# q and k loaded in quadrants of two heads, and transposed with an output step of two words

## The chip, the cores and the metric

The kernel runs on one core of a Trainium2 chip. The core has five engines with instruction queues of their own: TensorE (PE, matmuls; its weight loads are listed apart as PEld), VectorE (DVE), ScalarE (ACT), GpSimd (POOL) and SyncE (SP, which here only issues stores). Sixteen DMA engines move data between the chip's memory and the core's SBUF. Each engine runs its queue in order and waits at an instruction until what it needs is there. The metric is the device time of one execution in microseconds.

## What is computed

The reference is an attention with a sliding window and a bias by distance, followed by a gated layer.

```python
# q, k, v: (8 batches, 8 heads, 576 tokens, 64), float32
scores = scale * q @ k.T                      # scale = 1/8
bias   = slopes[h] * -abs(i - j)              # slopes[h] = 2 ** -(h + 1)
mask   = (i - j >= 0) & (i - j < 128)
attn   = softmax(where(mask, scores + bias, -1e9))
x      = (attn @ v).transpose(0, 2, 1, 3).reshape(4608, 512)
H = maximum(x @ w_h, 0)
T = sigmoid(x @ w_t + b_t)
out = T * H + (1 - T) * x                     # (4608, 512), float32
```

## The kernel before

**Units and blocks.** The attention is done in 32 *units* (b, s, g): a batch b, a set s of four of the eight heads, and a half g of the token range. The gated layer is done in 36 *blocks* of 128 rows and 512 columns; a block (b, 4) collects the first 64 tokens of two neighbouring batches.

**The order** is written out: the string ORDER has one letter for each step, and every engine's queue is filled in the order of that string. The steps of attention are L (a load, POOL issues it), T (a transpose of a loaded q or k tile, DVE, L184), s (scores, PE, L227), e (exponential, ACT, L244), m (multiplication by the mask, DVE, L249), p (probabilities times v, PE, L260, L268, L281) and n (division by the row sum, DVE, L294 and L295). Those of a block are x (transpose of x on PE, L321), c (its copy to SBUF, ACT, L326), h (projection with w_h, PE, L331), z (projection with w_t and a matmul that adds the bias, PE, L355 and L357) or w and y (bias copied by ACT, L368, then the projection alone, L372), r and u (relu and subtraction of x: r on ACT, L338, and u on DVE, L344, or both in one DVE step, L347), a (tanh, ACT, L377), t or k (to a gate, on ACT, L381, or DVE, L385), g (multiplication by the gate, DVE, L390), o or q (addition of x, on POOL, L394, or DVE, L399) and d (store, SP). S and M are the setup. The tuples RELU_ACT, GATE_DVE, BIAS_ACT and ADD_DVE say which blocks take which form, and LOADS in which order the 60 loads are issued.

**Loads.** All loads are issued by POOL and turn float32 into bfloat16 on the way. A load of q or k (L130) brings one batch and four consecutive heads: each of the 128 partitions holds one head's 18 consecutive tokens, in one piece of 4,608 bytes read. The tile has its own buffer out of 20. A load of v (L136) brings 128 tokens of 8 or 16 heads, in pieces of 64 numbers.

**Transposes.** Scores need q and k with the head dimension on the partitions. DVE transposes each tile in 18 squares of 32x32 words of 4 bytes (two bfloat16 numbers each). Square t takes token t of every partition's 18, so that its 32 results belong at words t, t + 18, t + 36 and so on of the output:

```python
out=TR[i % NTR][:]....rearrange("p (s t) -> p t s", t=NT),   # NT = 18
in_=LD[i % NLD][:].bitcast(U32).rearrange("p (t i) -> p t i", i=32)
```

**Masks.** The bias and the mask are applied in one of two ways. Most units multiply the exponentials by a table MT (step m). The units listed in MASK_PE have the distances added to the scores on PE instead (function distances, L209): four matmuls, one per head, of a scaled identity SI with a table of distances RB, each 128x128 with 384 or 448 columns; then m falls away.

**x.** The result of n is kept as x, two head sets after one another, with 64 numbers per head.

Of the kernel before, what the change touches and what calls it, by code (L numbers as in the profile page):

```python
# [11 lines left out]
NLD, NTR, NPB = 20, 12, 8  # L12


RELU_ACT = (0, 3, 5, 8, 9, 11, 12, 13, 17, 19, 20, 21, 26, 28)
GATE_DVE = (6, 7, 9, 15, 19, 23, 25, 26, 29, 32, 34)

LOADS = (0, 1, 3, 4, 6, 5, 2, 12, 11, 9, 13, 17, 10, 16, 8, 18, 7, 14, 21, 19, 15, 20, 22, 27, 26, 23, 25, 24, 29, 30, 31, 32, 33, 28, 34, 37, 39, 35, 40, 47, 38, 36, 43, 44, 45, 46, 48, 42, 41, 52, 56, 57, 50, 53, 58, 59, 51, 49, 55, 54)

BIAS_ACT = (8, 9, 14, 17, 20, 24, 30, 31, 32, 33, 34, 35)  # L20
ADD_DVE = (33, 35)

MASK_PE = (11, 14, 19)
# [3 lines left out]
    "SLLSMSLLLTLLTLs0LTLeLLTLMSms0Lp4LeLTLmLs0LTp6enLs0nLmx4Lex5Tp6cmcs0Lnz4b5eLTp6mas0tfnz4e"  # L27
    "Lh5mx6rh7cux5az6ucgtTp4oap6nLds0nLh4Th5eLx6x7uLrs0Tcz4Leumh5cmx6as0cuz7egTp4oh6anLtds0Lm"
    "rp4tLuez6ngz7gaoTtx6p4aLmdcs0x7eh6noTp4Ltds0cLnmh7euz4kw6gux5aos0Tch7eLdTp4Lynrs0akmp4w7"
    "eyugnh6oaTx4rs0LdtgLcgLp6gmx4Lz5cnex4oTp6cLds0unLz4eoTp6aLds0anoh5tTeh4dmz6rux7ah4kmcx5t"  # L30
    "p6ucgs0rnox5ez4TLdh6gLcmax7s0roTz5cw4Lgp6deuTyLts0naLaLgz4ueLTop6Tas0otdh5enh4dgux6oth7u"
    "cgx4w5dh6mctoyurTx4ap6dcms0z4euknh5agp6Ttos0th4neLduz6rmLLx7ap4mcs0np6egx4kh5nocs0ruLdx4"
    "gw5p6LmcyeuLnh4Tox6az7rmtLdp4ags0cgz7otneTz6odTx4aLds0cx5mah4w7uh6cgkeuyoup4gtds0maz6eon"
    "x7Tp4dcs0nh7eTh4h5autmp6rgs0uz5oenx4mdp6cs0uakz4engx5p6macs0onx4z5cdmeh4ggp6aoux5nh4odct"
    "z5krmdw4h6gauox7tx5uycgdkh6gaocx4h7ucodw6p4utydnw7ygagow6p4aytnodh7agdtx6ox4uh5ckw7dh6gc"
    "uoyw5uygdaqh4akdgtuogdqd"
# [36 lines left out]
def kernel(  # L73
# [38 lines left out]
    LD = [cp.tile([P, NT * D], BF16, name=f"ld{i}") for i in range(NLD)]  # L112
# [11 lines left out]
    RB = cp.tile([P, 448], BF16, name="rb")  # L124
    PS = pp.tile([P, 8, 512], F32, name="ps")

    def load(kind, *at):
        if kind == "t":
            b, s, w = at
            nc.gpsimd.dma_start(  # L130
                out=LD[(4 * b + 2 * s + w) % NLD][:],
                in_=(q, k)[w][b, 4 * s : 4 * s + 4].rearrange("h (p t) d -> (h p) (t d)", t=NT))
        elif kind == "v":
            b, n, m = at
            rows, h = min(P, S - m * P), b % 2 * H
# [320 lines left out]
```

## Time and profile before

| | |
|---|---|
| time, median of 3 runs | 151.55 us (150.25 to 152.34) |
| the profiled execution: time, span of its instructions | 151.79 us, 150.1 us |
| granted TensorE clock, mean | 0.987 of full speed |
| loads by the software DMA queue | 42,960 packets, 15.21 MB written |
| read from memory, written to it | 30.41 MB, 9.44 MB |
| q and k: 32 loads, landing after issue | 4.1 to 12.1 us, median 7.4 |
| wait of transposes for loads | 4.7 us in 5 waits, all before 31 us |

The span runs from the first to the last instruction; the time is 1.69 us longer. A page of the profile gives busy times of engines, the span in 40 slices, the chain of work that ended last (followed back from the last instruction, at each step to what released it or to the instruction before it on its engine), and groups of instructions by line with the mean duration of one and the idle time of the engine ahead of them. Lines such as L184 are lines of the kernel's file.

### The profile page before, as it was taken

How to read it: one execution, taken by the hardware profiler on the slowest of the kernel's cores; microseconds unless marked ns; L12 is line 12 of the kernel's file. 1: busy time of each engine (PE TensorE's matmuls, PEld its weight loads, DVE VectorE, ACT ScalarE, POOL GpSimd, SP SyncE). 2: the span in 40 equal slices, each digit the busy share in tenths (PEclk: the TensorE clock that was granted, in tenths of full speed). 3: DMA queues.
4: the chain of work that ended last, by engine and by line, in shares of the span. 5: the costliest groups of instructions: out<-in, count | busy, mean ns of one | idle time of the engine just before them, and what ended most of it. 6: DMA issues, size and time to landing. Idle time of an engine off the chain costs nothing.

```text
span 150.1 us, 5788 instructions
## 1 busy us (share of the span) xinstructions
PE 130.9 (87%) x2525; PEld 80.3 (54%) x2525; DVE 132.2 (88%) x226; ACT 119.3 (80%) x167; POOL 87.9 (59%) x102
## 2 busy tenths in 40 slices
PE   0477589969999999979999899997999999999960
PEld 0136465444666665655755556674557566555520
DVE  4974998759899999999969999999999999977882
ACT  5298369913999899769999979979799898899860
POOL 6977662195075851994159870859655035685640
PEclk9999999995999999999999999999999999999999
DMA  2999999999999999899999998399999121253544
GB/s 47 186 165 199 182 208 198 179 217 167 131 135 167 198 208 220 156 150 204 256 226 185 130 211 279 51 195 214 185 215 144 65 74 63 51 173 140 195 142 155
DMA packets 48233, 25.01 MB, mean 167 GB/s; under 512 B 38480, under 2 KB 39504, under 8 KB 48208
## 3 DMA queue, kind: packets, MB, share of 16 engines
q0 software_dynamic: 42960, 15.21, 96.6%
q1 hardware_dynamic: 5248, 9.44, 18.3%
q8 instruction: 19, 0.31, 0.9%
q14 instruction: 6, 0.05, 0.1%
HBM read 30.41 MB, written 9.44 MB: 266 GB/s over the span
## 4 chain that ended last, share of the span: by engine, by line
PE 46%; DVE 27%; DMA 17%; issue 3%; POOL 2%; ACT 2%; DVEq 0%; POOLq 0%; ACTq 0%
PE ps L331 14%; PE ps L355 8%; DMA va<-in_v_dram 8%; DVE x L295 6%; DVE p L249 6%; PE ps L372 6%; DMA ld<-in_q_dram 5%; DVE tr L184 5%; PE ps L227 5%; DMA ld<-in_k_dram 4%; PE ps L281 4%; DVE uu L390 3%; PE ps L321 3%; PE ps L260 3%; DVE uu L347 3%
## 5 line engine op out<-in xcount | busy, mean ns | idle before, releaser
L394 POOL TENSOR_TENSOR ot<-uu,x 128x512 f32<-128x512 bf16 x34 | 42.8, 1265 | 49.0 <-DVE uu L390 30.6
L244 ACT ACTIVATE p<-ps 128x1792 bf16<-128x1792 f32 (+1 forms) x32 | 50.0, 1562 | 12.2 <-PE ps L227 12.2
L184 DVE STREAM_TRANSPOSE tr<-ld 128x576 uint32<-128x576 uint32 x32 | 39.4, 1249 | 4.7 <-DMA ld<-in_q_dram 3.9
L331 PE MATMUL ps<-wH,xt 128*128 128x512 bf16 x144 | 37.3, 391 | 0.0
L249 DVE TENSOR_TENSOR p<-p,mt 128x1792 bf16<-128x1792 bf16 (+1 forms) x29 | 29.5, 1021 | 1.4 <-ACT p L244 1.4
L136 POOL DMA_DIRECT2D va<-in_v_dram x25 | 25.2, 1014 | 1.4 <-DMA ld<-in_q_dram 0.9
L295 DVE TENSOR_TENSOR x<-ps,rd 128x512 bf16<-128x512 f32 (+1 forms) x32 | 24.3, 758 | 1.3
L355 PE MATMUL ps<-wT,xt 128*128 128x512 bf16 x96 | 25.2, 386 | 0.0
L326 ACT COPY xt<-ps 128x512 bf16<-128x512 bf16 x36 | 21.0, 586 | 3.5 <-PE ps L321 3.3
L377 ACT ACTIVATE tt<-ps 128x512 f16<-128x512 f32 x36 | 21.5, 604 | 2.9 <-PE ps L372 1.6
L227 PE MATMUL ps<-tr,tr 32*64 32x192 bf16 (+2 forms) x1280 | 20.2, 248 | 1.3 <-DVE tr L184 1.3
L331 PEld LDWEIGHTS <-xt 128*128 128x128 bf16 x144 | 13.3, 100 | 14.3 <-issue 1.7
L227 PEld LDWEIGHTS <-tr 32*64 32x64 bf16 x1280 | 16.6, 112 | 6.6 <-DVE tr L184 2.9
L260 PE MATMUL ps<-va,p 128*128 128x65 bf16 x256 | 13.9, 198 | 4.7 <-DMA va<-in_v_dram 2.1
L260 PEld LDWEIGHTS <-p 128*128 128x128 bf16 x256 | 11.7, 100 | 9.4 <-DVE p L249 2.7
L347 DVE SCALAR_TENSOR_TENSOR uu<-ps,x 128x512 bf16<-128x512 f32 x22 | 14.9, 685 | 2.0 <-PE ps L331 1.8
L390 DVE TENSOR_TENSOR uu<-uu,tt 128x512 bf16<-128x512 bf16 x36 | 15.9, 454 | 0.2
L381 ACT ACTIVATE tt<-tt 128x512 f16<-128x512 f16 x25 | 15.7, 634 | 0.1
L321 PE MATMUL ps<-ident,x 128*128 128x128 bf16 x144 | 13.9, 224 | 2.0 <-DVE x L295 1.8
L321 PEld LDWEIGHTS <-x 128*128 128x128 bf16 x144 | 10.2, 99 | 8.7 <-issue 2.7
L281 PE MATMUL ps<-va,p 64*64 64x65 bf16 x448 | 14.7, 200 | 0.0
L355 PEld LDWEIGHTS <-xt 128*128 128x128 bf16 x96 | 8.2, 99 | 8.1 <-issue 0.8
(46 smaller groups left out, 116.8 us busy)
## 6 DMA issues: line engine op xcount, KB each, us to landing
out_dram<-ot SPq DMA_DIRECT2D x32, 256.0 KB, 4.1
ld<-in_q_dram POOLq DMA_DIRECT2D x16, 288.0 KB, 7.9
ld<-in_k_dram POOLq DMA_DIRECT2D x16, 288.0 KB, 7.2
va<-in_v_dram POOLq DMA_DIRECT2D x12, 256.0 KB, 7.7
va<-in_v_dram POOLq DMA_DIRECT2D x11, 128.0 KB, 7.9
out_dram<-ot SPq DMA_DIRECT2D x8, 128.0 KB, 2.8
wT<-in_moe_w_t_dram POOLq DMA_DIRECT2D x1, 512.0 KB, 8.9
wH<-in_moe_w_h_dram POOLq DMA_DIRECT2D x1, 512.0 KB, 10.8
```

The lines of the kernel that those rows point to most:

```text
L136: nc.gpsimd.dma_start(out=VA[b // 2][0:rows, h : h + n * H, m, 0:D], in_=v[b : b + n, :, m * P : m * P + rows].rearrange("b h p d -> p (b ...
L184: nc.vector.transpose(out=TR[i % NTR][:].rearrange("p s e -> p (s e)").bitcast(U32).rearrange("p (s t) -> p t s", t=NT), in_=LD[i % NLD][: ...
L227: nc.tensor.matmul(out=PS[r * D : r * D + D, bank + a, c0:c1], lhsT=KT[row : row + 32, k0 : k0 + D, e], rhs=QT[row : row + 32, q0 : q0 + c ...
L244: nc.scalar.activation(out=PB[i][:, :, 0:w], in_=PS[:, bank : bank + 4, 0:w], func=ACTF.Exp, scale=scale)
L249: nc.vector.tensor_tensor(out=p[:, :, 0:w], in0=p[:, :, 0:w], in1=MT[s][:, :, 448 - w : 448] if g else MT[s][:], op=ALU.mult)
L260: nc.tensor.matmul(out=PS[:, bank + o, a * E : a * E + E], lhsT=p[:, a, col : col + P], rhs=VA[b // 2][:, b % 2 * H + 4 * s + a, i, :], st ...
L295: nc.vector.tensor_tensor(out=X[b, g][:, s, :, 0:n, :], in0=av[:, :, 0:n, 0:D], in1=rd[:, :, 0:n, :].to_broadcast([P, 2, n, D]), op=ALU.mult)
L321: nc.tensor.transpose(out=XP[b, i][:, c * P : (c + 1) * P], in_=xchunk(b, i, c), identity=ident[:])
L331: nc.tensor.matmul(out=pa, lhsT=XT[b, i][:, c, :], rhs=wH[:, c, :], start=c == 0, stop=c == NC - 1)
L355: nc.tensor.matmul(out=pz, lhsT=xt[:, c, :], rhs=wT[:, c, :], start=c == 0, stop=False)
L377: nc.scalar.activation(out=tt[:], in_=PZ.pop((b, i)), func=ACTF.Tanh, scale=0.5)
L394: nc.gpsimd.tensor_tensor(out=like(ot[:], i), in0=like(UU.pop((b, i))[:], i), in1=xview(b, i), op=ALU.add)
```

## The change

From batch 2 on (NBW = 2) a load of q or k is made of two DMAs. Each brings two heads into one quadrant of 32 partitions: partition p of the quadrant gets, of both heads, the token pairs 2p and 2p + 1 of each run of 64 tokens, nine pairs per head, each pair a piece of 512 bytes read and 256 written. The buffers now hold both halves of the heads of a batch (10 buffers twice as long); half s of a buffer holds heads 2a + s in quadrant a. A load fills two quadrants, both halves, so each of a batch's transposes reads what two loads brought. In a square, the 32 results of a transpose lie two words apart. For batches 0 and 1 the pieces and the squares stay as they were, with heads 2a + s instead of 4s + a.

With this a head set s has the heads 2a + s; the v tiles and SI are indexed so, and x is kept with both sets beside one another, so that a block's 512 columns are contiguous.

The distances are added by up to 20 matmuls of 64x64 instead of four of 128x128, over those columns of each 64-row part that the scores use, and RB has 256 columns. Seven units instead of three use them, two of them the first two units. The lists give 11 blocks instead of 14 to r on ACT, 10 instead of 12 to w and y, 3 instead of 2 to q, and 11 to k as before. ORDER and LOADS are new throughout.

```diff
-NLD, NTR, NPB = 20, 12, 8
+NLD, NTR, NPB, NBW = 20, 12, 8, 2
-RELU_ACT = (0, 3, 5, 8, 9, 11, 12, 13, 17, 19, 20, 21, 26, 28)
-GATE_DVE = (6, 7, 9, 15, 19, 23, 25, 26, 29, 32, 34)
+RELU_ACT = (4, 6, 7, 8, 9, 10, 16, 23, 24, 25, 30)
+GATE_DVE = (4, 8, 9, 13, 15, 16, 19, 24, 29, 32, 33)
...
-BIAS_ACT = (8, 9, 14, 17, 20, 24, 30, 31, 32, 33, 34, 35)
-ADD_DVE = (33, 35)
-MASK_PE = (11, 14, 19)
+BIAS_ACT = (9, 13, 14, 19, 26, 30, 32, 33, 34, 35)
+ADD_DVE = (32, 33, 35)
+MASK_PE = (0, 1, 9, 11, 15, 16, 23)
...
-    LD = [cp.tile([P, NT * D], BF16, name=f"ld{i}") for i in range(NLD)]
+    LD = [cp.tile([P, NS, NT * D], BF16, name=f"ld{i}") for i in range(NLD // 2)]
...
             b, s, w = at
-            nc.gpsimd.dma_start(
-                out=LD[(4 * b + 2 * s + w) % NLD][:],
-                in_=(q, k)[w][b, 4 * s : 4 * s + 4].rearrange("h (p t) d -> (h p) (t d)", t=NT))
+            ld, src = LD[(2 * b + w) % (NLD // 2)], (q, k)[w][b]
+            if b < NBW:
+                nc.gpsimd.dma_start(
+                    out=ld[:, s, :],
+                    in_=src.rearrange("(h s) (p t) d -> s h p (t d)", s=NS, t=NT)[s])
+                return
+            for a in (2 * s, 2 * s + 1):
+                nc.gpsimd.dma_start(
+                    out=ld[32 * a : 32 * a + 32, :, :].rearrange("p s (t x) -> p (s t) x", x=2 * D),
+                    in_=src[2 * a : 2 * a + 2].rearrange("h (t p j) d -> p (h t) (j d)", p=32, j=2))
...
     def tr(b, s, w):
         i = 4 * b + 2 * s + w
-        nc.vector.transpose(
-            out=TR[i % NTR][:].rearrange("p s e -> p (s e)").bitcast(U32).rearrange(
-                "p (s t) -> p t s", t=NT),
-            in_=LD[i % NLD][:].bitcast(U32).rearrange("p (t i) -> p t i", i=32))
+        to = TR[i % NTR][:].rearrange("p s e -> p (s e)").bitcast(U32)
+        ld = LD[(2 * b + w) % (NLD // 2)][:, s, :].bitcast(U32)
+        if b < NBW:
+            nc.vector.transpose(out=to.rearrange("p (s t) -> p t s", t=NT),
+                                in_=ld.rearrange("p (t i) -> p t i", i=32))
+        else:
+            nc.vector.transpose(out=to.rearrange("p (t s j) -> p t j s", s=32, j=2),
+                                in_=ld.rearrange("p (t j i) -> p t j i", j=2, i=32))
...
     def distances(s, g, bank):
-        w = width(g)
-        for a in range(4):
-            nc.tensor.matmul(out=PS[:, bank + a, 0:w], lhsT=SI[:, 4 * s + a, :],
-                             rhs=RB[:, 448 - w : 448], start=True, stop=False,
-                             skip_group_check=True)
+        steps, parts = tiles(g)
+        for n, step in enumerate(steps):
+            for a0 in (0, 2):
+                for i, r in step:
+                    c0, c1, k0, q0 = parts[i, r]
+                    at = D + q0 - k0
+                    if k0 == D:
+                        c0, at = 0, 0
+                    for a in (a0, a0 + 1):
+                        row = a % 2 * D
+                        nc.tensor.matmul(
+                            out=PS[r * D : r * D + D, bank + a, c0:c1],
+                            lhsT=SI[row : row + D, 2 * a + s, row : row + D],
+                            rhs=RB[row : row + D, at : at + c1 - c0], start=n == 0,
+                            stop=False, tile_position=(row, r * D), skip_group_check=True)
...
-            X[b, g] = xp.tile([P, NS, 2, 6, D], BF16, name="x")
+            X[b, g] = xp.tile([P, 2, 6, NS, D], BF16, name="x")
...
-            out=X[b, g][:, s, :, 0:n, :], in0=av[:, :, 0:n, 0:D],
+            out=X[b, g][:, :, 0:n, s, :], in0=av[:, :, 0:n, 0:D],
```

## The prediction

> **What bounds the kernel now.** I read the page's busy times and slices first, then the busy times in stretches of 10 us, then the chain, and last the POOL queue in order of time.
>
> The page, on busy time and in 40 slices of 3.75 us (tenths busy):
>
> ```profile
> PE 130.9 (87%) x2525; PEld 80.3 (54%) x2525; DVE 132.2 (88%) x226; ACT 119.3 (80%) x167; POOL 87.9 (59%) x102
> ...
> PE   0477589969999999979999899997999999999960
> ...
> DVE  4974998759899999999969999999999999977882
> ...
> DMA  2999999999999999899999998399999121253544
> ```
>
> Three things are full at once. PE and DVE are, from slice 10 to slice 34, and the DMA engines are until slice 30. Busy time on PE overstates its work, so I price PE by the chain, where matmuls run back to back:
>
> ```profile
> 19.75 11.87 DMA va<-in_v_dram
> 31.67 0.30 PE ps L260 x4
> ...
> 80.27 0.65 PE ps L209 x4
> ...
> 83.33 0.53 PE ps L227 x40
> ...
> 108.14 0.86 PE ps L355 x4
> 109.00 0.22 PE ps L357
> ...
> 112.87 0.24 PE ps L260 x8
> 113.12 0.37 PE ps L281 x12
> ...
> 131.01 0.86 PE ps L331 x4
> ...
> 144.09 0.88 PE ps L331 x4
> ```
>
> Columns are start, length, what. PE waits for a load of v until 31.67, ends its last projection at 144.97, and a DVE and store tail ends the span at 150.1. A projection costs 0.86 (with a bias matmul 1.08), a unit of scores 0.53 or 0.47, a unit of p times v 0.61 (0.86 with the shared block), the transposes of a block 0.25 (0.22 to 0.33), four distance matmuls 0.65. By the groups of PE in 0 to 31.6 us, what is left at 31.67 is 34 h (29.2), 21 z (22.7), 12 y (10.4), 32 x (8.0), 26 s (13.0), 28 p (19.1) and 3 distances (2.0): **104.4 us of work in 113.3 us**. So PE stalls for only 8.9 us. The chain runs on DVE from 38.5 to 65 and from 90.5 to 104.3; by the same prices these stretches hold 24.6 us of PE work in 26.5 and 12.2 in 13.8. Relieving DVE there can give 3.5 us.
>
> **The change, part by part.**
>
> *Transposes.* Groups by form:
>
> ```profile
> L184 DVE STREAM_TRANSPOSE tr<-ld 128x576 uint32<-128x576 uint32 x32 | 39.4, 1249 | 4.7 <-DMA ld<-in_q_dram 3.9 <-DMA ld<-in_k_dram 0.9
> L249 DVE TENSOR_TENSOR p<-p,mt 128x1792 bf16<-128x1792 bf16 x16 | 17.3, 1080 | 0.9 <-ACT p L244 0.9
> L295 DVE TENSOR_TENSOR x<-ps,rd 128x512 bf16<-128x512 f32 x24 | 16.6, 692 | 1.0
> L295 DVE TENSOR_TENSOR x<-ps,rd 128x768 bf16<-128x768 f32 x8 | 7.7, 958 | 0.3
> ```
>
> The two forms of L295 give 266 ns for 256 more elements, 1.04 ns each, and 160 ns fixed. A transpose at this slope would take 759 ns; it takes 1249. Either its output step of 18 words costs the other 490 ns, or the operation itself does. With a step of two words 24 of the 32 fall between 0.54 us (the slope of DVE's memsets, 165 ns for 128 elements and 272 for 256, plus its fixed 58 ns) and 1.25 us (nothing gained; the step shrinks, so I see no reason for more). I take 0.72, near the L295 slope: 24 x 0.53 = 12.7 us off DVE, bounds 0 and 17.
>
> Two rules of the Trainium skill oppose each other here. "SBUF — State Buffer" (Door 1, on cachelines) has lines of 16 bytes and wants two hits in each; a step of two words gives two, and 24 transposes at the full rate would save what I took. "Vector Engine (DVE) Microarchitecture Reference" (5.2) gives the full rate only to runs of two adjacent words; a two-word step has none, and by this rule of the Trainium skill the transposes stay at 1249 ns, the first rival below. The row of 1249 ns agrees with both.
>
> *Masks and small moves.* Seven units instead of three get their mask on PE: 4 x 1.02 (between the two forms of L249, 1.08 and 0.95) = 4.1 us off DVE. Three relus move from ACT plus L344 (483 ns) to L347 (685): +0.6; one add moves from POOL: +0.7. DVE in all: 132.2 - 12.7 - 4.1 + 1.3 = **116.7 us**. ACT loses three relus (603 each) and two bias copies (596): -3.0. The new layout of x keeps sizes and types; I take it as nothing.
>
> *Distances on PE.* Twenty 64x64 matmuls instead of four of 128x128. Ends: half a unit of scores (40 small matmuls in 0.5), 0.25, and the old 0.65. I take 0.5, nearest to a unit of scores because the tiles may run side by side. Two of the seven lie before 31 us, in the DMA's shadow. What is left for PE from the first p of batch 1 on, by the new order: 34 h 29.2, 24 z 25.9, 10 y 8.8, 32 x 8.0, 25 s 12.5, 28 p 19.1, 5 distances 2.5: **106.0 us**.
>
> *Start.* That p waited for the 21st load and now for the 20th, with one q/k load fewer ahead (1.4 us). But PE had caught up only 1.49 us before, and has some 0.6 us more to do, at the start's slower pace: resume at 31.0 instead of 31.67.
>
> *Loads.* This is the part that can hurt. In the queue on POOL:
>
> ```profile
> 10.55 0.54 POOL L130 DMA_DIRECT2D ld<-in_q_dram  x1 [0.92 <-DMA ld<-in_k_dram]
> ...
> 31.01 4.33 POOL L136 DMA_DIRECT2D va<-in_v_dram  x4
> ```
>
> 24 loads become 48, each of 576 pieces of 512 bytes read and 256 written, where a load had 128 pieces. An issue takes 0.56 us with 128 pieces, 1.17 with the 2048 of a v load: by the line between, 0.70 with 576. POOL gets 24 x (1.40 - 0.57) = +20 us, less one add (1.27): about 107 of 147. Its idle time (49 us ahead of L394, 31 of it waiting for DVE) hides that as long as adds and loads are not queued behind one another. At 10.55 and every later stall of the start, the issue waits for the landing of the eighth DMA before it; with two DMAs per load that is four loads in flight, not eight, and adds queue behind the wait.
>
> Time on the DMA engines: consecutive landings at the start lie 1.3 to 1.7 us apart for q/k (I use 1.4), 0.9 for a v load of 1024 pieces, 14 ns a piece and engine (1024/16 = 64), up to 18 ns with 2048 pieces in 2.3 us. By bytes alone 512-byte pieces change nothing: 1.4. If a piece costs per byte as two v pieces, 72 x 36 ns = 2.6. I take 1.65, nearer the bytes, since a v piece exceeds its bytes' time (9.8 ns at q/k's rate, 8 rows of 4,608 bytes per engine in 1.4 us) by 4 to 8 ns and so one of 512 bytes takes 24 to 28, at 72 per engine 1.7 to 2.0, or 1.4 if the two overlap. That is +6 us over the run (0 to 29). "SBUF — State Buffer" (Door 1) of the Trainium skill has 189 GB/s for a DMA on 32 partitions; as an estimate from it, 0.295 MB would take 1.56 us a load, and no row here shows such a DMA.
>
> What hides it: the landings of 45 to 116 us leave about 9 us in which nothing is in flight or only one load's latency runs (93.4 to 100.4 and around 46). What is late next if the cover goes: each transpose of a batch now waits for both loads of its tensor, behind it stand DVE's masks, norms and gates, and PE's scores wait for it.
>
> **Sum.** 31.0 + 106.0 + stalls + tail 5.1. Of the old 8.9 us of stalls I take away DVE's 3.5 and the 1.4 of the DVE pieces at 85.8 to 87.7, and keep 4.0. Span 146.1; the profiled run had 151.79 for a span of 150.1, so 147.8; it stands 0.24 over the median, so **147.6** against 151.55, 2.6% faster. Two per cent (148.5 to 154.6) is about what a measurement of this kernel can tell from no change.
>
> **The rivals.**
> 1. *Transposes stay long* (the step is not their cost). DVE keeps 129.4 and its two stretches; only 4.1 us of masks are lighter, half of that on the chain, less 1.6 us of PE work: 150 to 152. For it: nothing in the trace separates step from operation, and the memsets of va with a step of 130 bytes (80 elements in 125 ns) show no penalty. Against: the 490 ns over the slope of other rows have no other visible source.
> 2. *Freed DVE time turns into other stalls* (ACT 90% busy in mid-run, POOL's longer queue): stalls stay near 8.9, 31.0 + 106.0 + 8.9 + 5.1 + 1.7 = 152.7, or 149 with half of it.
> 3. *The loads become the bound: slower.* The place is the queue of loads from 32 us to the last v, behind which, in the new order, 28 us of PE work (from the p of batch 6 that needs it) and the tail follow. The 9 us of slack are used up from 9/24 = 0.4 us extra per load; at +0.6 it is 5 us late, against the 4 us gained elsewhere, so about 153; at +1.2 it is 20 us late, 168. POOL's limit of eight works in the same way. For it: DMA busy 9 to slice 30, and landings 6 to 12 us after issue. Against: until 116 us few transposes waited (4.7 us, all at the start), and the new order issues batch 3 earlier.
>
> **How the numbers follow.** Forecast (145 to 148.5): 0.42. Rivals 1 and 2, within 2%: 0.13 and 0.14. Rival 3: 0.31, mostly 154.6 to 162. The range 144.5 to 159 leaves out the best end (transposes at 0.54, no stalls) and the far end of rival 3.
>
> **What will show it.** L184 in two kinds, 1.25 us x8 and near 0.7 x24; L130 with 56 issues, the new near 0.7 us; distances at 0.5 a unit; the chain nearly all PE after 31 us. Waits of the transposes for ld beyond the start, POOL waiting for DMAs in mid-run, or v landing after PE wants it would make the prediction wrong on the slow side; L184 unchanged would make it wrong towards no change.

## The result, and the profile after

The changed kernel takes 172.09 us, median of 4 runs (170.89 to 177.39), against 151.30 us for the kernel before, measured beside it (150.25 to 152.34). Run against run the ratio is 1.135, with a 95% interval of 1.123 to 1.146: 13.5% slower, where 2.6% faster was forecast and the range ended at 159. The profiled execution has a span of 169.2 us (before 150.1), at a granted clock of 0.97. Medians below hold all runs of a kernel; the ratios leave out disturbed executions, so that the two can differ by a per cent.

Busy times, slices (now of 4.23 us) and the queue of loads, from the page of the changed kernel:

```profile
PE 132.1 (78%) x2656; PEld 85.1 (50%) x2687; DVE 127.4 (75%) x221; ACT 117.5 (69%) x162; POOL 106.0 (63%) x124
...
PE   0405660799939996689979999999799999999960
...
DVE  3337009577918799558959999999998998898892
...
DMA  1799999999999999999969999999999811233536
...
q0 software_dynamic: 70992, 15.22, 146.9%
```

PE was nearly full from slice 10 on. It now has holes until slice 21 (89 us) and a smaller one at slice 29, DVE has two empty slices at 17 to 25 us, and the DMA engines have next to no slack until slice 31. The same bytes come in 70,992 packets instead of 42,960.

The chain that ended last, in order of time (start, length, what):

```profile
3.96 10.93 DMA ld<-in_q_dram
15.18 11.71 DMA va<-in_v_dram
27.17 12.60 DMA va<-in_v_dram
40.05 9.65 DMA va<-in_v_dram
...
63.29 1.48 issue
...
70.41 2.02 issue
...
84.91 1.02 issue
```

Before, too, loads of v handed over to one another, the last ended at 31.67 us, and PE worked from there. Now a load of q and three of v do, and the last of these holds PE until 49.70 us. From there to the end of the span it is 119.5 us; from 31.67 us in the kernel before it was 118.4. **What was lost lies before 50 us**; the lighter DVE shows as no gain behind it. The three pieces called "issue" are new as well: PE idle with nothing that the profile shows to wait for.

Groups by form (busy us, mean ns of one, then the idle time ahead of it), of the changed kernel:

```profile
L192 DVE STREAM_TRANSPOSE tr<-ld 128x576 uint32<-128x576 uint32 x24 | 17.7, 758 | 4.5 <-DMA ld<-in_q_dram 4.3 <-DMA va<-in_v_dram 0.2
...
L137 POOL DMA_DIRECT2D ld<-in_q_dram x24 | 16.0, 669 | 5.2 <-DMA va<-in_v_dram 3.1 <-DMA wH<-in_moe_w_h_dram 1.2 <-DMA ld<-in_k_dram 0.8
...
L189 DVE STREAM_TRANSPOSE tr<-ld 128x576 uint32<-128x576 uint32 x8 | 9.7, 1253 | 16.9 <-DMA ld<-in_q_dram 16.4 <-DMA ld<-in_k_dram 0.5
...
L397 DVE TENSOR_SCALAR tt<-tt 128x512 f16<-128x512 f16 x11 | 7.3, 664 | 0.7 <-ACT tt L389 0.7
```

The 24 short transposes take 758 ns and a new issue 669 ns, both close to their forecast. The eight long transposes of batches 0 and 1, which the change hardly touches, wait 16.4 us for loads of q.

### The profile page after: what moved, and what is told of

Read it like the earlier page. It is cut to its first block, busy times and chain, and to the rows that moved or that the text cites. A ratio compares the mean times of both kernels' runs of the same rounds, so it can differ in the third digit from the quotient of the medians.

```text
span 169.2 us, 6109 instructions
## 1 busy us (share of the span) xinstructions
PE 132.1 (78%) x2656; PEld 85.1 (50%) x2687; DVE 127.4 (75%) x221; ACT 117.5 (69%) x162; POOL 106.0 (63%) x124
## 3 DMA queue, kind: packets, MB, share of 16 engines
q0 software_dynamic: 70992, 15.22, 146.9%
## 4 chain that ended last, share of the span: by engine, by line
PE 54%; DMA 27%; issue 8%; DVE 7%; POOL 1%; ACT 0%; DVEq 0%; POOLq 0%
DMA va<-in_v_dram 20%; PE ps L343 15%; PE ps L367 11%; PE ps L243 7%; DMA ld<-in_q_dram 6%; PE ps L297 6%; PE ps L333 5%; PE ps L276 4%; PE ps L369 3%; PE ps L384 2%; DVE tr L192 2%; DVE uu L359 2%; DVE uu L402 1%; PE ps L223 1%; DVE ot L411 1%
## 5 line engine op out<-in xcount | busy, mean ns | idle before, releaser
L406 POOL TENSOR_TENSOR ot<-uu,x 128x512 f32<-128x512 bf16 x33 | 41.0, 1246 | 32.3 <-DVE uu L402 20.0
L343 PE MATMUL ps<-wH,xt 128*128 128x512 bf16 x132 | 36.1, 387 | 0.7 <-issue 0.2
L265 DVE TENSOR_TENSOR p<-p,mt 128x1536 bf16<-128x1536 bf16 (+1 forms) x25 | 27.7, 1110 | 1.5 <-ACT p L260 1.5
L367 PE MATMUL ps<-wT,xt 128*128 128x512 bf16 x88 | 27.3, 403 | 1.2 <-issue 0.4
L189 DVE STREAM_TRANSPOSE tr<-ld 128x576 uint32<-128x576 uint32 x8 | 9.7, 1253 | 16.9 <-DMA ld<-in_q_dram 16.4
L192 DVE STREAM_TRANSPOSE tr<-ld 128x576 uint32<-128x576 uint32 x24 | 17.7, 758 | 4.5 <-DMA ld<-in_q_dram 4.3
L137 POOL DMA_DIRECT2D ld<-in_k_dram x24 | 15.8, 662 | 6.8 <-DMA ld<-in_q_dram 3.5
L343 PEld LDWEIGHTS <-xt 128*128 128x128 bf16 x144 | 13.0, 99 | 12.9 <-issue 0.8
L137 POOL DMA_DIRECT2D ld<-in_q_dram x24 | 16.0, 669 | 5.2 <-DMA va<-in_v_dram 3.1
L359 DVE SCALAR_TENSOR_TENSOR uu<-ps,x 128x512 bf16<-128x512 f32 x25 | 16.9, 677 | 1.4 <-PE ps L343 0.8
L402 DVE TENSOR_TENSOR uu<-uu,tt 128x512 bf16<-128x512 bf16 x36 | 17.2, 485 | 0.2
```

What stands on the lines that cost most here:

```text
L137: nc.gpsimd.dma_start(out=ld[32 * a : 32 * a + 32, :, :].rearrange("p s (t x) -> p (s t) x", x=2 * D), in_=src[2 * a : 2 * a + 2].rearrang ...
L265: nc.vector.tensor_tensor(out=p[:, :, 0:w], in0=p[:, :, 0:w], in1=MT[s][:, :, 448 - w : 448] if g else MT[s][:], op=ALU.mult)
L343: nc.tensor.matmul(out=pa, lhsT=XT[b, i][:, c, :], rhs=wH[:, c, :], start=c == 0, stop=c == NC - 1)
L367: nc.tensor.matmul(out=pz, lhsT=xt[:, c, :], rhs=wT[:, c, :], start=c == 0, stop=False)
L406: nc.gpsimd.tensor_tensor(out=like(ot[:], i), in0=like(UU.pop((b, i))[:], i), in1=xview(b, i), op=ALU.add)
```

## The experiments

Ratios are against the kernel before measured beside each, with their 95% intervals. The first question was the start.

**a_contig.** The changed kernel, batches 0 and 1 with four consecutive heads per load.

```diff
-                    in_=src.rearrange("(h s) (p t) d -> s h p (t d)", s=NS, t=NT)[s])
+                    in_=src[4 * s : 4 * s + 4].rearrange("h (p t) d -> (h p) (t d)", t=NT))
```

> The changed kernel, but loads of q and k of batches 0 and 1 take four consecutive heads again (the heads of these two batches end up in another order, so the result isn't the reference's; all sizes and counts stay). Theory A: the time went at the start, because a load of every second head is cut into four rows of heads that don't follow one another, and lands late (the first load 9.3 us after its issue, before 4.1; the first p of batch 1 at 41 us instead of 31.7). Then the first load lands after about 4.1 us, PE resumes at 31 to 36 us, and the time falls from 172 to 156 to 163. Theory B: the start is late because of the quadrant loads that stand ahead of the v loads of batch 1, eight DMAs in flight at a time. Then the first load may land early, but PE still waits near 47 to 50 us, and the time stays above 167.

161.89 us, ratio 1.068 (1.048 to 1.087): **10.2 us of the loss go with one line of the load.** The first transpose on DVE's timeline, of the changed kernel and then of this one (start, length):

```profile
10.69 1.26 DVE L189 STREAM_TRANSPOSE tr<-ld 128x576 uint32<-128x576 uint32 x1 [4.70 <-DMA ld<-in_q_dram]
```

```profile
5.65 2.65 DVE L189 STREAM_TRANSPOSE tr<-ld 128x576 uint32<-128x576 uint32 x2
```

Both loads were issued at 1.33 us. With strided heads the first lands 9.3 us later, with consecutive ones 4.3 (4.1 in the kernel before). The p of batch 1 on PE's timeline, in the changed kernel and in this one:

```profile
41.13 0.41 PE L276 MATMUL ps<-va,p 128*128 128x65 bf16 x8
...
49.74 0.35 PE L276 MATMUL ps<-va,p 128*128 128x65 bf16 x4 [2.79 <-DMA va<-in_v_dram]
```

```profile
31.83 0.42 PE L276 MATMUL ps<-va,p 128*128 128x65 bf16 x8
...
38.92 0.28 PE L276 MATMUL ps<-va,p 128*128 128x65 bf16 x4 [1.26 <-DMA va<-in_v_dram]
```

The first p comes 9.3 us earlier, the one that waits for v 10.8.

**b_strided.** The other way round: the kernel before, with every second head in batches 0 and 1.

```diff
-                in_=(q, k)[w][b, 4 * s : 4 * s + 4].rearrange("h (p t) d -> (h p) (t d)", t=NT))
+                in_=((q, k)[w][b].rearrange("(h s) (p t) d -> s h p (t d)", s=NS, t=NT)[s] if b < 2 else
+                     (q, k)[w][b, 4 * s : 4 * s + 4].rearrange("h (p t) d -> (h p) (t d)", t=NT)))
```

> The kernel before, with only the loads of q and k of batches 0 and 1 taking every second head (the heads of these batches are in another order, so the result isn't the reference's). Theory A: the first load lands after about 9 us instead of 4.1, PE resumes 8 to 12 us later than 31.7, time 159 to 164. Theory B: nothing of this, 150 to 154.

160.96 us, ratio 1.076 (1.061 to 1.092). The eight loads alone cost the kernel before about what they cost the changed one (7.6% here, 6.7% between a_contig and the changed kernel). The stretch of 0 to 10 us (from, length, busy times, then clock, DMA share, GB/s), of the kernel before and of this one:

```profile
0.00:10.00 10.00, 3.31 (x47) 1.70 (x48) 7.09 (x19) 5.41 (x11) 8.37 (x19) 1.00 0.87 130
```

```profile
0.00:10.00 10.00, 1.65 (x4) 0.51 (x4) 3.60 (x16) 4.65 (x10) 7.29 (x16) 1.00 0.51 69
```

The load does not keep the DMA engines busier: their share falls to 0.51, and what they move to 69 GB/s. The queue's packets in the stretch of 4 to 6 us (number, MB, the time that they took as a share of 16 engines), of the kernel before and of this one, where the first four loads have been issued by 4.5 us:

```profile
q0 software_dynamic: 195, 0.38, 109.0%
```

```profile
q0 software_dynamic: 191, 0.13, 49.6%
```

As many packets move a third of the bytes, for 133 of the 191 are under 512 bytes (28 of 195 before). The whole run has 3,072 packets more, 384 per strided load, all under 512 bytes. What these small packets add to the delay was not tried apart from the gap.

The row of 0.51 fits a rule of the Trainium skill, "DMA: Bandwidth & Descriptors" (Why a DMA increments its semaphore by 16 and not by 1, on the number of engines): a DMA is spread over the largest number of engines, 16 at most, that divides the slowest dimension of both its patterns. Four strided heads cannot be merged with the 32 partitions of each, so that this dimension is 4, where consecutive heads make one of 128. By this rule of the Trainium skill a load would have a quarter of the engines, and two loads at once half of them, which is the size of the 0.51 and the 49.6%. No run here names the engines or shows how many loads move at a time.

**a_quadbig.** The changed kernel, batches 0 and 1 brought by quadrant too, in whole pieces of 4,608 bytes: two DMAs per load, 32 partitions each, both halves of the heads.

```diff
             if b < NBW:
-                nc.gpsimd.dma_start(
-                    out=ld[:, s, :],
-                    in_=src.rearrange("(h s) (p t) d -> s h p (t d)", s=NS, t=NT)[s])
+                for a in (2 * s, 2 * s + 1):
+                    nc.gpsimd.dma_start(
+                        out=ld[32 * a : 32 * a + 32, :, :],
+                        in_=src[2 * a : 2 * a + 2].rearrange("h (p t) d -> p h (t d)", t=NT))
                 return
```

> The changed kernel, with the loads of batches 0 and 1 also made by quadrant (two DMAs of 32 partitions and two heads each), but in whole pieces of 4,608 bytes; nothing is left out. Theory A: with 32 partitions as the outer dimension nothing is cut into four, so the first tile is complete about 5 to 7 us after its issue, PE resumes at 32 to 38 us, time 156 to 164. If DMAs of 32 partitions are themselves the slow thing: first landing still near 9 us, 167 or more.

166.2 us, ratio 1.096 (1.082 to 1.110). Its first DMA lands 3.1 us after issue, so pieces in another order of dimensions are not slow. But a tile needs both loads of its tensor, and the first tile is complete at 10.5 us, as in the changed kernel (10.7); 5 to 7 us after the issue had been expected. Some 6 of the 10 us come back, which puts the time between the two expectations: it speaks for neither alone.

**b_heads.** The kernel before, with the strided heads of batches 0 and 1 brought by one DMA per head.

```diff
+            if b < 2:
+                for a in range(4):
+                    nc.gpsimd.dma_start(
+                        out=LD[i][32 * a : 32 * a + 32, :],
+                        in_=(q, k)[w][b, 2 * a + s].rearrange("(p t) d -> p (t d)", t=NT))
+                return
```

> The kernel before, with the same tiles in batches 0 and 1 as the changed kernel has there (heads 2a + s), but brought by four DMAs per load, one for each head, 32 partitions in whole pieces of 4,608 bytes. Only the loads of those two batches change, and v stays with heads 4s + a, so the output of batches 0 and 1 is not the reference's. Theory: what made the strided load slow (first landing 9.2 us after issue, 160.96 us in all) is that one DMA steps over a gap between four heads, and that such a DMA keeps few packets in flight; with one DMA per head nothing steps over a gap. The first tile is then complete some 4.5 to 6 us after its first issue (three more issues of 0.57 us than one load has), and the kernel takes 151 to 155 us, the loss being POOL's 24 issues more and its limit of eight in flight. Rival: reading every second head is what costs, wherever the gap stands. Then the first tile is complete only after 9 us or more, and the time stays at 159 us or above.

The mechanism came as the theory has it, the time did not. Each of the four DMAs lands 2.4 to 2.6 us after its issue, and the first tile is complete 4.1 us after its first issue, as in the kernel before: the gap inside one DMA was the trouble, not the heads. But the kernel takes 164.69 us, ratio 1.079 (1.070 to 1.089), a time that the rival had forecast, though the late first tile that it rested on did not come. What I had left out of the sum is on POOL's timeline, first of the kernel before, then of this one:

```profile
4.63 2.67 POOL L136 DMA_DIRECT2D va<-in_v_dram  x3
```

```profile
1.33 2.17 POOL L133 DMA_DIRECT2D ld<-in_q_dram  x4 [0.82 <-POOLq L447]
3.49 1.95 POOL L133 DMA_DIRECT2D ld<-in_k_dram  x4
...
10.39 2.68 POOL L143 DMA_DIRECT2D va<-in_v_dram  x3
```

An issue costs POOL 0.5 us, and 24 more put 12 us of issuing into a start in which nothing hides it. The first loads of v go out 5.8 us later, and the group of four that goes out at 31.01 us in the kernel before goes out at 41.75.

**a_heads4.** The changed kernel with one DMA per head in batches 0 to 3, quadrants from batch 4 on.

```diff
-NLD, NTR, NPB, NBW = 20, 12, 8, 2
+NLD, NTR, NPB, NBW = 20, 12, 8, 4
...
-                nc.gpsimd.dma_start(
-                    out=ld[:, s, :],
-                    in_=src.rearrange("(h s) (p t) d -> s h p (t d)", s=NS, t=NT)[s])
+                for a in range(4):
+                    nc.gpsimd.dma_start(
+                        out=ld[32 * a : 32 * a + 32, s, :],
+                        in_=src[2 * a + s].rearrange("(p t) d -> p (t d)", t=NT))
```

> The changed kernel, mended by what the runs have shown: batches 0 to 3 are loaded in whole pieces of 4,608 bytes with one DMA per head and transposed at 18 words, and quadrants and two-word transposes begin with batch 4. Nothing is left out. With four consecutive heads in place of every second one this took 155.9 us. Theory (each loss is where it was found: the gap between heads 10 us, the quadrants of batches 2 and 3 6 us): 155.5 to 159 us, the upper end for 48 more issues on POOL while loads are dense. Rival (every second head is slow in any form): 164 us or more. Neither expects it to beat the kernel before.

172.22 us, ratio 1.128 (1.119 to 1.138): a miss by 13 us, for the reason just seen. L133 has 64 issues of 0.5 us, POOL is 121.7 us busy, and "POOL ld L133" alone is 12% of the chain. The mend is as bad as the fault.

The second question was the quadrants.

**a_nbw4.** a_contig, with quadrants and two-word steps only from batch 4 on.

```diff
-NLD, NTR, NPB, NBW = 20, 12, 8, 2
+NLD, NTR, NPB, NBW = 20, 12, 8, 4
```

> The changed kernel with consecutive heads in the whole loads, and quadrant loads and two-word transposes only from batch 4 on instead of batch 2 (the result isn't the reference's: batches 0 to 3 have their heads in another order). 24 quadrant DMAs are left out of 48; eight transposes are 0.5 us longer. If the loss sits where loads are dense (batches 2 and 3, 30 to 60 us): 151 to 155. If each quadrant load costs the same wherever it is: about 157. If the order is the cause: 160 or more.

**a_whole.** a_contig, all loads whole; the transposes of batches 2 to 7 keep the two-word step.

```diff
-            if b < NBW:
-                nc.gpsimd.dma_start(
-                    out=ld[:, s, :],
-                    in_=src[4 * s : 4 * s + 4].rearrange("h (p t) d -> (h p) (t d)", t=NT))
-                return
-            for a in (2 * s, 2 * s + 1):
-                ...
+            nc.gpsimd.dma_start(
+                out=ld[:, s, :],
+                in_=src[4 * s : 4 * s + 4].rearrange("h (p t) d -> (h p) (t d)", t=NT))
```

> The changed kernel, with all loads of q and k made as before the change (one DMA, 128 pieces, four consecutive heads), and nothing else undone: order, distances, layout of x and the two-word transposes stay (heads and tokens end up in another order, so the result isn't the reference's). Against the run with consecutive heads in batches 0 and 1 only (161.9 us) it takes away the quadrant loads alone. Theory A: the rest of the loss, about 10 us, is the quadrant loads (48 DMAs of small pieces, which crowd the DMA engines from 30 to 60 us and hold up v, the transposes and even PE's instructions): 149 to 153, no stall of PE over 1 us in the middle of a unit. Theory B: it is the new order: 157 or more.

a_nbw4 takes 155.9 us, ratio 1.031 (1.022 to 1.040); a_whole 154.92 us, ratio 1.024 (1.015 to 1.033). So the quadrants of batches 2 and 3, which are loaded at 20 to 55 us when the DMA engines are full, cost 3.7% (1.068 to 1.031), some 6 us; and that although a_nbw4 also makes eight more transposes 0.5 us longer each. The 32 DMAs of batches 4 to 7 cost about 1 us by the medians, which the intervals do not separate from nothing. Both times lie between their two expectations, and against theory A a_whole still has stops of PE without a named cause, 4.4 us together; the fourth question is about these.

**steps.** The price of a transpose, in one run (167.52 us): every load by quadrant, the output step (and the piece read) another one in each batch.

```diff
+STEP = (18, 18, 1, 2, 3, 6, 9, 18)
...
+        j = STEP[b]
+        nc.vector.transpose(out=to.rearrange("p (t s j) -> p t j s", s=32, j=j),
+                            in_=ld.rearrange("p (t j i) -> p t j i", j=j, i=32))
```

> A measurement: the changed kernel with every load by quadrant, and per batch another number of tokens per piece, so another output step of the transposes: 18 words in batches 0, 1 and 7, and 1, 2, 3, 6 and 9 words in batches 2 to 6; nothing is left out. If a transpose is slow because each word written lies in another line of 16 bytes: 0.75 us at 1 and 2 words, between at 3 (one or two words per line), 1.25 at 6 and more. If it is slow unless two words are adjacent: 0.75 at 1 only, and 2 would not differ from 3. Loads by the distance of their landings: 2.3 to 2.8 us with pieces of 256 bytes, 1.5 to 1.7 with 512, 1.4 to 1.6 above.

DVE's timeline of this kernel, one line for each of the steps 1, 2, 3, 6, 9, 18:

```profile
46.82 0.77 DVE L186 STREAM_TRANSPOSE tr<-ld 128x576 uint32<-128x576 uint32 x1
...
61.34 0.77 DVE L186 STREAM_TRANSPOSE tr<-ld 128x576 uint32<-128x576 uint32 x1
...
72.81 0.95 DVE L186 STREAM_TRANSPOSE tr<-ld 128x576 uint32<-128x576 uint32 x1
...
86.01 1.23 DVE L186 STREAM_TRANSPOSE tr<-ld 128x576 uint32<-128x576 uint32 x1
...
107.38 1.22 DVE L186 STREAM_TRANSPOSE tr<-ld 128x576 uint32<-128x576 uint32 x1
...
125.70 1.25 DVE L186 STREAM_TRANSPOSE tr<-ld 128x576 uint32<-128x576 uint32 x1
```

One word and two cost the same, three cost 0.18 us more, six and more 0.45 to 0.48. That settles, for these transposes, the prediction's two opposed rules: the one of "SBUF — State Buffer" (Door 1, lines of 16 bytes, two hits in each) in the Trainium skill agrees, since steps of one and two words put two or more results in a line, three words sometimes, six never. The rule of adjacent pairs from "Vector Engine (DVE) Microarchitecture Reference" (5.2) does not hold for them.

The landings did not come as expected. Pieces of 256 bytes read (batch 2) land 1.8 to 2.1 us apart per load, where 2.3 to 2.8 was expected; those of 512 (batch 3) 1.9 to 2.2, where it was 1.5 to 1.7; the larger ones of batches 4 and 6 1.5 to 1.7. In the changed kernel pieces of 512 bytes land 1.8 us apart at 50 to 60 us and 1.6 to 1.7 at 74 to 80 us. So the stretch in which a load moves matters about as much as its pieces do.

The third question: what is 12 us less on DVE worth?

**b_step2.** The kernel before, all 32 transposes at a step of two words, nothing else.

```diff
-                "p (s t) -> p t s", t=NT),
-            in_=LD[i % NLD][:].bitcast(U32).rearrange("p (t i) -> p t i", i=32))
+                "p (t s j) -> p t j s", s=32, j=2),
+            in_=LD[i % NLD][:].bitcast(U32).rearrange("p (t j i) -> p t j i", j=2, i=32))
```

> The kernel before, with only the output of the 32 transposes written at a step of two words (the loads are as before, so tokens come out in another order and the result isn't the reference's). It takes 32 x 0.51 = 16 us off DVE and nothing else. The forecast's step (DVE relief is worth 3.5 to 5 us on the chain): 146 to 149. Rival 2 (freed DVE time turns into other stalls): 150 to 152.

150.38 us, ratio 0.999 (0.992 to 1.005). DVE is busy 122.4 us instead of 132.2, and the time is the same. By the interval the relief is worth 1.2 us at most. The 16 us that were expected off DVE became 9.8: the transposes gave 15, but its other work grew by 5 (the masks of 1,792 columns, for one, from 1080 to 1186 ns).

**a_long.** The reverse, in the order of the changed kernel: a_whole with all transposes long.

```diff
-NLD, NTR, NPB, NBW = 20, 12, 8, 2
+NLD, NTR, NPB, NBW = 20, 12, 8, 8
```

> The changed kernel with the loads of all batches whole (four consecutive heads) and all 32 transposes written at the long step of 18 words: of the change there remain the order, the masks on PE, the distances and the layout of x. The output is not the reference's, since the loads' heads are not those that v is indexed by. Beside it stands the same kernel with two-word transposes in batches 2 to 7, at 154.92 us. Theory (relief of DVE is worth next to nothing, since other waits take its place): 154 to 157 us, though DVE has 24 x 0.5 = 12 us more to do. Rival (the new order is made for the lighter DVE, and the short transposes earn what the prediction gave them, 4 to 5 us): 159 us or more.

159.54 us, ratio 1.037 (1.029 to 1.046), against 1.024 for a_whole. By the medians the short transposes earn 4.6 us there, by the ratios 1.4% (2 us), and the two intervals overlap. It lies between the two expectations: that the new order profits from them is likely, not shown, and by the ratios it is less than the prediction's 4.9 us.

The fourth question: a_whole has whole loads and short transposes, and is still 2.4% slower than the kernel before. Why?

**a_oldorder.** a_whole with ORDER, LOADS and the lists of the kernel before (so three units with distances instead of seven).

> The same as the run with whole loads, but with ORDER, LOADS and the lists of the kernel before; it keeps the small distances, the layout of x and the two-word transposes (the result isn't the reference's, as there). If these parts cost nothing: 148 to 151, as the kernel before with two-word transposes (150.4). If the new layout or the 64x64 distances cost something: 152 or more. The difference to the run with whole loads is the new order alone: under theory A within 3 us, under theory B 6 us or more.

**a_olddist.** The same, with the distances by four 128x128 matmuls again; what is left of the change is the layout of x and 24 short transposes. The table RB has its 448 columns and its setup of before again, here and in a_wholeold.

```diff
-        steps, parts = tiles(g)
-        for n, step in enumerate(steps):
-            ...
+        w = width(g)
+        for a in range(4):
+            nc.tensor.matmul(out=PS[:, bank + a, 0:w], lhsT=SI[:, 2 * a + s, :],
+                             rhs=RB[:, 448 - w : 448], start=True, stop=False,
+                             skip_group_check=True)
```

> The kernel with whole loads, two-word transposes and the order of before (154.33 us), with the distances added again by four 128x128 matmuls. As there, loads bring four consecutive heads while v and the scaled identity are indexed for every second one, so the output is not the reference's. What is left of the change is the layout of x and the two-word step. Theory: the remaining loss against the kernel before (1.5 per cent) comes from the 64x64 distances (200 or so PE instructions more, 80 fewer here) and the stalls of PE at each 256th instruction that lie behind them; then 150 to 151.5 us. Rival: it comes from the layout of x (PE's transposes and DVE's normalisation read and write other strides); then 153.5 to 155 us, as without this edit. The kernel before in the same call decides between them: within 1 per cent of it for the theory, 1.5 per cent or more over it for the rival.

a_oldorder takes 154.33 us, ratio 1.015 (1.003 to 1.027); a_olddist 150.44 us, ratio 0.994 (0.990 to 0.999). Between a_whole and a_oldorder lie 0.9%, which the intervals do not separate from nothing. The layout of x costs nothing that shows, and the 64x64 distances cost 2% (0.4 to 3.7 by the ends of the intervals), in only three units and the two of the setup. By PE's own price (0.45 to 0.5 us a unit in the chain, against 0.65) they should have gained. On PE's timeline of a_oldorder there are two idle times for which the profile names no cause:

```profile
20.00 0.48 PE L237 MATMUL ps<-tr,tr 32*64 32x128 bf16 x17 [1.12 <-issue]
...
51.72 0.33 PE L237 MATMUL ps<-tr,tr 32*64 32x128 bf16 x10 [1.71 <-issue]
```

In a_olddist and in the kernel before there is none over 0.3 us. Counted along PE's matmuls and weight loads in the traces, such a stop stands, in every kernel that has them, within three instructions of number 192 + 256n: at the edges of blocks of 256. The queue of instructions on the page (packets, MB, share), of the kernel before and of the changed one, has packets of 16 KB, and as many as PE has such blocks:

```profile
q8 instruction: 19, 0.31, 0.9%
```

```profile
q8 instruction: 21, 0.34, 1.0%
```

**b_shift.** The kernel before, with 64 small matmuls (each with its weight load) at the start, while PE has nothing to do: all later instructions stand half a block further on.

```diff
+PAD = 64
...
+            for _ in range(PAD):
+                nc.tensor.matmul(out=PS[0:D, 4, 0:16], lhsT=ident[0:D, 0:D], rhs=ident[0:D, 0:16],
+                                 start=True, stop=False, tile_position=(0, 0), skip_group_check=True)
```

> The kernel before with the same 64 small matmuls at the start; nothing else is changed. If stalls of PE at each 256th instruction depend on where these fall, some should appear here, where there are none now: 152 to 155 us, with idle times of PE for nothing of 0.5 us and more at instructions half a block from the old places. If the kernel before is free of them because it has fewer PE instructions where the DMA engines are full, none appears and the time is that of the kernel before within 1 per cent.

155.27 us, ratio 1.014 (1.007 to 1.022). Four lines of PE's timeline, where the kernel before has none such:

```profile
45.33 0.31 PE L285 MATMUL ps<-va,p 64*64 64x65 bf16 x8 [1.89 <-issue]
...
63.63 0.22 PE L285 MATMUL ps<-va,p 64*64 64x65 bf16 x3 [0.66 <-issue]
...
71.19 0.43 PE L231 MATMUL ps<-tr,tr 32*64 32x192 bf16 x25 [1.92 <-issue]
...
105.23 0.37 PE L264 MATMUL ps<-va,p 128*128 128x65 bf16 x7 [1.29 <-issue]
```

5.8 us of stops, and 1.4% more time, for matmuls that delay nothing by themselves: **where the 256th instructions fall matters.** All lie before 116 us, when the loads still fill the DMA engines. A padding by a whole block of 256, which would move every edge by one block and leave the stops where they were, was not tried.

Which edges stop PE can be read from the start and length that the traces hold of each q8 packet. Each packet starts after PE has passed an edge: up to 5.8 us after it while loads are queued, at most 1.3 us after it once the last load has landed. Each of the 33 stops over 0.3 us in these kernels ends 1.2 to 1.8 us after the end of the packet that followed the edge before; at the edges without a stop PE never arrives earlier than 1.16 us after that end. In the changed kernel, for one, PE passes an edge at 64.8 us, the packet runs from 70.2 to 71.1, PE stands at the next edge from 70.4 and goes on at 72.4. So PE stops where its work between two edges is shorter than the packet's way. This is how the traces read; no experiment changed the packet's way alone. One order of instructions can stop or not: b_step2, with the instructions of the kernel before on PE, has one stop of 1.17 us at 85.6 us, where that kernel has none.

**a_shift.** a_oldorder with the same 64 matmuls.

> The kernel with whole loads, two-word transposes and the order of before (154.33 us), with 64 small matmuls (64x64 by 16 columns) more at the start, while PE waits for the first load: every later instruction stands 128 places, half a block, further on in PE's stream. They write a place that is overwritten later; the heads are as in that kernel. Theory A (what counts is where the 256th instructions fall): the two stalls of PE for nothing at 20.0 and 51.7 us (1.1 and 1.7 us) go or move to other instructions, and the time changes with them, to 150.5 to 153 us if none takes their place. Theory B (the number of instructions in a stretch counts, not the places): stalls of together 2.5 to 4 us remain, at other places, and 153.5 to 155.5 us. Rival C (the 64x64 distances are dear by themselves): stalls or not, 153.5 to 155.5 us.

155.3 us (152.6 to 156.4). Its two stops moved, to 45.2 and 51.7 us, and shrank from 2.8 to 2.0 us; the time is the same within the scatter. It does not separate theory B from rival C.

**a_wholeold.** a_whole with the old distances in all seven units.

> The changed kernel with all loads whole and two-word transposes (154.92 us) and the distances added by four 128x128 matmuls in all seven units: of the change there remain the order, the choice of masks, the layout of x and the two-word step. As there, loads bring four consecutive heads while v is indexed for every second one, so the output is not the reference's. By PE's own price the old distances are dearer (0.65 against 0.5 us, seven times: +1 us). Theory: the 64x64 distances cost in another way, by 160 matmuls and 160 weight loads more in PE's instruction stream and the stalls at each 256th instruction (some 5 us in that kernel, none in the one with the order of before and old distances); then 150 to 152.5 us, with no such stall longer than 0.5 us. Rival: the stalls belong to the new order, or the loss to its waits; then 154.5 to 157 us.

155.04 us, ratio 1.012 (1.000 to 1.025). The stops, 4.4 us together in a_whole, are all gone, and by the ratios 1.1% with them, which the intervals do not separate from nothing. PE's waits for x on DVE grow from 0.9 to 3.1 us instead; those for masks stay (2.3 us, 2.4 in a_whole). So the theory holds for the stops and fails for the time: in the new order other waits take most of their place.

## Why the prediction was wrong

**The step that failed first is "Start".** It kept the loads of batches 0 and 1 as they were, priced only their number, and had PE resume at 31.0 us. PE's first p of batch 1 came at 41.1 and its chain began at 49.7. a_contig shows that the rest of this step was right (31.8), and that the whole error is a changed source pattern in a line of the diff that I had taken as none: "the pieces and the squares stay as they were" is true of the size of a piece, but the four heads of a load no longer follow one another in memory, and it lands 9.3 us after its issue instead of 4.1. The trace of before showed no load with a gap between heads; I should have bounded it like the other unseen rows.

**"Loads", the third rival, happened, in the place where it was put and for less than half of the loss.** The sizes were good: 0.70 us an issue (measured 0.67), POOL at about 107 us (106.0), 1.65 us of DMA time per load (in a dense stretch, quadrants land 0.7 to 1.0 us apart, 1.5 to 1.9 per load). The slack was not: I took it as 9 us spread over 24 loads. The loads of batches 2 and 3 have none (6 us lost), those of 4 to 7 have enough (1 us).

**"Relieving DVE there can give 3.5 us", and the 1.4 with it, failed.** This is the second rival. The transposes went to 0.758 us (forecast 0.72), and b_step2 shows at most 1.2 us for it in the order of before; a_long shows 2 to 4.6 us in the new one. DVE itself came to 127.4 us instead of 116.7. Eleven gates L397 take 664 ns each instead of 303 (4.0 us), the 25 masks cost 27.8 us and so save 1.8 instead of 4.1, L402 takes 485 ns instead of 454 (1.1 us), and the transposes are 0.9 us over; the rest of the 10.7 us was not traced. The gate of the kernel before, beside the line of L397 shown above:

```profile
L385 DVE TENSOR_SCALAR tt<-tt 128x512 f16<-128x512 f16 x11 | 3.3, 303 | 0.0
```

The gates are long where POOL works beside them. In the changed kernel four of the eleven take about 1.24 us, three about 0.4 and four 0.28 to 0.30. The seven long ones began while POOL ran an addition or issued a load, and six of them end 0.15 to 0.16 us after that addition does. Three long masks (2.04, 2.36 and 1.15 us), which make the 2.3 us of the masks, lie beside POOL instructions likewise. In a_oldorder the same gate takes 303 ns, in a_whole, with the order of the changed kernel, 402. So the new order and its loads put POOL's work beside these steps; this too is read from the traces, and no experiment tried it.

**"Distances" had the right price and missed what comes with it.** A unit takes 0.45 to 0.5 us. But 160 more matmuls with their weight loads (180 instead of 20) move the edges of PE's blocks of 256 instructions into places where PE stops: 4.5 us of it in the changed kernel, at 64.8, 72.4 and 85.9 us. With the old order the old distances gain 2%; with the new one they gain 1.1% or nothing. What is left of a_wholeold's 1.2% is open.

"x" as nothing was right (a_olddist). Rival 1 is out: the transposes did become short. Two slips of the working change nothing in it: ten y at 0.86 us are 8.6, not 8.8, and the slope of the memsets, which set only a bound, runs from a row of bfloat16 to one of uint32.

By the ratios the loss goes: 13.5% in all, 6.7 for the strided heads, 3.7 for the quadrants of batches 2 and 3, 0.7 for the others, 2.4 left with whole loads (order, distances and masks together, after what the short transposes give back). Each share is a difference of two ratios, and known to within 1 to 2.

## What to carry to other kernels

Price a load by its access pattern, not by its bytes and its pieces: four strided heads as the outermost dimension of a load halved the rate of the start here (130 to 69 GB/s), and splitting it into more DMAs costs as much again in issues while nothing hides them. Ask of an engine's relief which wait ends next; 10 us off an engine that is 88% busy bought nothing measurable. And an edit that changes the number of instructions on a dense engine can cost or gain 1 to 2% by where its blocks of 256 fall, so compare such edits with more than one padding.

## What was not expected of the hardware

- A DMA of four heads of 32 partitions with gaps between them lands 9.2 us after issue instead of 4.1, at a share of the DMA engines of 0.51 against 0.87 in the first 10 us. A gap alone does not do it: the DMAs of a_quadbig, whose outermost dimension is 32 partitions, land in 3.1 us.
- PE stops for 0.3 to 3.25 us (the longest in a_contig at 57.9 us) at some of its 256-instruction edges while loads are queued; after the last load has landed only one is seen, of 0.47 us (a_quadbig, 131.1 us). The Trainium skill, "Runtime: NRT & Kernel Launch" (Instruction fetch mechanics), has the blocks of 256 instructions, fetched ahead by DMA, and calls the cost of an edge mostly hidden; the rows here agree with the blocks and differ on the cost. An edge stops PE when PE reaches it before, or less than 1.2 us after, the end of the packet that started behind the edge before. More and smaller matmuls reach it sooner.
- After some waits PE is granted a clock of 0.5 for 3.4 us: in the changed kernel from 49.8 us, after the wait of 2.79, and from 73.7 us, soon after the stop of 2.02; in the kernel before from 33.6 us, after a wait of 1.49. It does not follow each: in b_shift the stop of 1.92 us at 71.2 has it behind it, and the one of 1.89 us at 45.3 has not. In a_heads4, which has the emptiest start, it is 0.50 in the whole stretch of 20 to 30 us. What this costs was not priced.
- A gate on DVE that began beside an addition on POOL takes up to 1.24 us instead of 0.30, and most such gates end 0.10 to 0.16 us after the addition.
- A transpose's price depends on its output step: 0.77 us for one or two words, 0.95 for three, 1.22 to 1.25 for six and more.
